# A third open unit of VectorE's exponentials, the table of softmax sums in DRAM, and four weight loads set three tiles apart

## The chip, the cores and the metric

The kernel runs on one core of a Trainium2 chip. The metric is the device time of one execution in microseconds. The engines are TensorE (PE in the profile, with its weight loads as PEld), VectorE (DVE), ScalarE (ACT), GpSimd (POOL) and SyncE (SP), which issues all of the kernel's DMAs from one queue, in program order.

## The reference

One transformer block without biases, in bf16, with 2048 rows of 640 columns, 32 heads of 20 columns and a gated linear part of 1728 columns:

```python
def _A_ref(x, wqkv, wo):
    qkv = (x @ wqkv).reshape(B, S, 3, H, Dh).transpose(2, 0, 3, 1, 4)
    q, k, v = qkv[0], qkv[1], qkv[2]
    scores = jnp.einsum("bhqd,bhkd->bhqk", q, k) * (Dh ** -0.5)
    p = _softmax(scores, axis=-1)
    o = jnp.einsum("bhqk,bhkd->bhqd", p, v)
    return o.transpose(0, 2, 1, 3).reshape(B, S, D) @ wo
def _B_ref(x, w_gate, w_up, w_down):
    h = jnp.einsum("bsd,df->bsf", x, w_gate) * jnp.einsum("bsd,df->bsf", x, w_up)
    return jnp.einsum("bsf,fd->bsd", h, w_down)
x = A_x
h = x + _A_ref(_layernorm(x), A_wqkv, A_wo)
h2 = h + _B_ref(_layernorm(h), B_w_gate, B_w_up, B_w_down)
```

The largest single piece is the exponential of the scores: 32 heads times 2048 times 2048 elements.

## The kernel before, in words

**A written order.** The instruction order on every engine is made at build time. A planner in the kernel keeps modelled times of PE, ACT and DVE (`at["pe"]`, `at["exp"]`, `at["dve"]`) and emits instructions by them. The chip then executes each engine's list in order, with semaphores between the engines.

**Score tiles.** The attention is cut into 683 tiles of up to 1536 score columns (three PSUM banks of 512; two tiles of this kind, `sc`, are in flight). `emit_S` (L577) lets PE make the scores (L591), and ACT takes the exponential of the tile into `E` or `El` (L607). `emit_AV` (L794) multiplies the exponentials with the values, two tiles or more behind (L828), and collects them in one accumulator `acc`. A "segment" is what one accumulator collects: four heads for a block of 512 or 256 query rows. When it is complete, VectorE copies it to an `asb` buffer (L840, three buffers) or adds it to a part (L845).

**Units.** `x_takes` (L627) decides, tile by tile, whether VectorE computes the last bank of the tile in place of ACT; ACT then has 1024 columns instead of 1536. Such a unit is four VectorE instructions on 128x512 elements: `xv<-sc` (L644), which reads the scores, then two polynomial steps `xt` (L654, L655) and `xe` (L649), which gives the exponentials to the AV products. `emit_x` (L636) emits the first at once and puts the other three into `x_open`; `spare` and `step_x` emit these later, between VectorE's other work, as its modelled time allows. With several units open `x_next` alternates between the first two in the list. A unit is taken only if fewer than two units are open, fewer than five are unconsumed (`X_OUT`), VectorE's modelled time is not far behind PE's, and the tile isn't among the last of its segment.

**Work between the tiles.** Projections, the output product, the gated part (`job_glu`) and the down product (`job_y`) are generators that PE runs in the gaps between the tiles; each ends with a VectorE instruction that empties the one PSUM bank `mi`. Where PE has no such work the planner emits matmuls whose result isn't used (`keep_warm`, L509). Layernorm pieces for VectorE wait in the queues `aux` and `hot`. The attention covers the query blocks in turn, and the gated part of each block runs during the attention of the next. The last 256 rows are done after the attention, in `last_tail`.

**Softmax sums.** The sums are rows of the `asb` buffer. `norm` (L693) writes them to DRAM (L700), reads them back spread over 128 partitions into a slice of the SBUF table `sums_all` (L701, 128x512 f32), takes reciprocals (L711), writes these to DRAM (L713) and reads them back broadcast into `bc` (L716); later VectorE multiplies (L719). For eight segments `job_norm` and `last_tail` make the reciprocals by way of PE (`sums_to_rows`, L737) and copy the sums into the table (L745). At the end `flag_ok` (L1468) reduces the whole table (L1471, L1472), to see that all sums were in range.

**The last weights.** When the gated part of the last block's first half has been emitted, `load_last` (L1389) loads the rows of the last 256 positions (`xr`, L1072, 2 x 160 KB) and the first two pairs of weight tiles (`wu`, `wg`, L1202, 4 x 320 KB), one after the other on SP's queue. They are used in `last_tail`.

Of the kernel before, what the change touches and what calls it, by code (L numbers as in the profile page):

```python
# [66 lines left out]
TURN_NS, TURN_FROM = 4200, 2  # L67
HOLD_AT, HOLD_NS = 5300, 450
AV_ROUNDS, AV_LATE, X_LATE = 2, 3, 0
GAP_NS, FILL_LEAST = 250, 300  # L70
FULL_IN, FULL_NS, ALL_NS = 2083, 300, 760
X_LEAST, X_OUT, X_SOON = 2, 5, 4
X_CHUNK = 3
PE_NS = {"out": 6000, "glu": 23000, "y": 7000}
NF_NS = 1800
ALONE_NS = {"out": 4350, "glu": 15260, "y": 5710}
# [16 lines left out]
def kernel(  # L93
# [43 lines left out]
    half = const.tile([P, TPB], F32, name="half")  # L137
    wo = [const.tile([P, D], BF16, name=f"wo{g}") for g in range(NG)]
    N_SUMS = 16 * (NB * NG)
    sums_all = const.tile([P, N_SUMS], F32, name="sums_all")  # L140

    qa = [qkp.tile([P, QA], BF16, name=f"qa{g}", tag=f"qa{g}") for g in range(NG)]
    qb = [qkp.tile([P, QB], BF16, name=f"qb{g}") for g in range(NG)]
# [218 lines left out]
    x_open = deque()  # L362
    x_last = [None]
    holds = deque()
    x_left = {}
    x_put = []
    x_live = deque()
# [30 lines left out]
    def later(n, fn):  # L398
        events.append((now["i"] + n, fn))
# [73 lines left out]
    def spare(until):  # L473
        while True:
            soon = x_open and last_tile[x_open[0][0]] - now["i"] <= X_SOON
            if at["dve"] + (x_next()[0] if soon or x_open and not aux else 600) > until + TOL:
                break
            if step_aux(hot):
                continue
            if soon:  # L480
                step_x()
            elif not step_aux() and not step_x():
                break
# [143 lines left out]
    def x_takes(i):  # L627
        us, n = tiles[i]
        s = us[-1][0]
        whole = segs[s][4] == "only"  # L630
        if not whole and (aux or last_tile[s] - i < X_CHUNK):
            return False
        return (n == EW and (PASS[segs[s][0]][0] < LAST_B or room()) and last_tile[s] - i >= X_LEAST and len({u[0] for u in us if not whole and u[3] >= n - BANK or whole}) == 1
                and len(x_open) < 2 and at["dve"] < at["pe"] + PE_DVE + TOL and len(x_live) < X_OUT)

    def emit_x(ps, us):  # L636
        s = us[0][0]
        w = PASS[segs[s][0]][2]
        v = xp.tile([P, BANK], F32, name="xv", bufs=2)
        u = v[:].bitcast(U16).rearrange("p (n h) -> p n h", h=2)[:, :, 0]  # L640
        t = xp.tile([P, BANK], F32, name="xt", bufs=2)
        e = xp.tile([P, BANK], I16, name="xe", bufs=X_OUT)
        dve(608, 0)
        took = nc.vector.tensor_scalar(v[:], ps, X_SCALE, X_BASE, ALU.mult, ALU.max)  # L644
        x_live.append((s, us[-1][1], us[-1][2]))
        x_left[s] = x_left.get(s, 0) + 1

        def last():
            nc.vector.scalar_tensor_tensor(e[:], t[:], X_R, v[:], ALU.mult, ALU.add)  # L649
# [3 lines left out]
        x_open.append((s, deque([  # L653
            lambda: nc.vector.scalar_tensor_tensor(t[:], u, X_P, u, ALU.add, ALU.mult),  # L654
            lambda: nc.vector.scalar_tensor_tensor(t[:], t[:], X_Q, u, ALU.add, ALU.mult),  # L655
            last])))
        x_last[0] = x_open[-1]
        return took
# [31 lines left out]
    def read_out(b):  # L690
        return all(("om", b, t) in done for t in TAILS[b])

    def norm(s, asb):  # L693
        p, g = segs[s][0:2]
        b, c0, w = PASS[p]
        n = w // 32
        r16 = sums_all[:, col["n"]:col["n"] + n]
        col["n"] += n
        sums = dram.tile([HPG, w], F32, name="sums", tag=f"sums{w}")
        nc.sync.dma_start(sums[:], asb[DH:P:SLOT, 0:w])  # L700
        nc.sync.dma_start(r16, sums[:].rearrange("j (c f) -> (j c) f", f=n))  # L701

        due = at["dve"] + SUMS_NS

        def back():
            if at["pe"] < due and now["i"] < n_tiles:
                later(1, back)
                return
            ri = nrm.tile([P, n], F32, name="ri", tag=f"ri{n}")
            dve(130)  # L710
            nc.vector.reciprocal(ri[:], r16)  # L711
# [6 lines left out]
            def times(asb, bc, p, g, c0, w):  # L718
                nc.vector.tensor_tensor(On[g][:, c0:c0 + w], asb[:, 0:w], bc[:, 0:w], ALU.mult)  # L719
# [14 lines left out]
            nc.tensor.matmul(ps[:, HPG * t:HPG * (t + 1)], lhsT=asb[:, t * P:(t + 1) * P], rhs=identf[:, DH:P:SLOT], start=True, stop=True)  # L734
        return ps

    def sums_to_rows(ps, w):  # L737
        n = w // SLOT
        r16 = sums_all[:, col["n"]:col["n"] + n]
        col["n"] += n  # L740
# [4 lines left out]
        nc.vector.tensor_copy(r16, ps[:, 0:n])  # L745
        return bc

    def rows_to_cols(bc, w, ps):
# [4 lines left out]
    def job_norm(s, asb):  # L753
        p, g = segs[s][0:2]
        b, c0, w = PASS[p]
        ps = sums_on_pe(asb, w)
        yield 780 * w // QB
        dve(700, 0)
        bc = sums_to_rows(ps, w)
# [5 lines left out]
        nc.vector.tensor_tensor(On[g][:, c0:c0 + w], asb[:, 0:w], ps[:, 0:w], ALU.mult)  # L765
        done.add(("n", p, g))
        yield NEXT

# [25 lines left out]
    def emit_AV(upto):  # L794
# [41 lines left out]
        if acc["left"] == 0:  # L836
            dve(605 if w == QB else 342, 0)
            if kind in ("copy", "only"):
                asb = parts[g] if kind == "copy" else nrm.tile([P, QB], F32, name="asb", bufs=3)
                nc.vector.tensor_copy(asb[:, 0:w], acc["t"][:, 0:w])  # L840
                if kind == "copy":
                    part[g] = asb
            else:
                asb = part[g]
                nc.vector.tensor_tensor(asb[:, 0:w], acc["t"][:, 0:w], asb[:, 0:w], ALU.add)  # L845
            acc["seg"], acc["from"], at["acc"] = None, now["i"] + 2, at["dend"] + DVE_PE
            if s == FINAL:
                final["asb"] = asb
            elif (p, g) in FAST:
                opens["nf", p, g] = at["dend"] + DVE_PE  # L850
                urgent.append((("nf", p, g), job_norm(s, asb)))
            elif kind in ("only", "last"):
                norm(s, asb)
# [535 lines left out]
    def load_last():  # L1389
        st = tail_st[LAST_B]  # L1390
        load_tail(st, LAST_T)
        load_w(0, st)
        load_w(1, st)

    def run(gen):
        for _ in gen:
# [2 lines left out]
    def last_tail():  # L1399
# [16 lines left out]
                                 rhs=wo[NG - 1][:, hf * HALF:(hf + 1) * HALF], start=False, stop=True)  # L1416
        ta, tb = LAST_T
        out_most(ta, 0)
        bc = sums_to_rows(sums_on_pe(asb, HW), HW)
        out_most(ta, 1)  # L1420
        ps = rows_to_cols(bc, HW, accp.tile([P, QB], F32, name="acc"))
        for k in range(2):
# [41 lines left out]
    def fill():  # L1464
        while step() is not None:
            pass

    def flag_ok():  # L1468
        n = col["n"]
        bits = sums_all[:, 0:n].bitcast(I32)  # L1470
        nc.vector.tensor_reduce(ext[:, 0:1], bits, axis=AX.X, op=ALU.min)  # L1471
# [165 lines left out]
```

## Time and profile before

| | |
|---|---|
| median of 3 runs | 899.88 us (899.21 to 900.29) |
| the profiled execution | 895.79 us |
| its span from first to last instruction | 893.9 us |
| mean granted TensorE clock | 0.997 |
| busy in the span | PE 836.4 us, DVE 778.4, ACT 851.4, POOL 31.5 |
| tiles' exponentials on ACT (L607) | 683 instructions, 482 with 1536 columns or less than a full tile, 201 with 1024 |
| units on VectorE (L644) | 201 |

Durations are those of the profiled execution, whose time is 4.09 us below the median of the runs. In groups of instructions a line gives the engine, the operation, output and input by the program's names, shapes and the count, then busy time in us and the mean in ns, then the engine's idle time just before these instructions with what ended most of it. A timeline row gives start and duration in us, with the idle time before it in brackets; a row with a count stands for several neighbouring instructions, shown with the shape of the first. PEclk is the granted TensorE clock as a share of full speed.

### The profile page before, as it was taken

Reading aid. Unit: us, or ns where it says so; the run is one execution under the profiler, and the core shown is the slowest. Engines: PE = TensorE matmul, PEld = TensorE weight load, DVE = VectorE, ACT = ScalarE, POOL = GpSimd, SP = SyncE. Lnnn points to the kernel's source line nnn. Section 1 sums busy time; section 2 is a strip of 40 time slices with the busy share of each in tenths; the row PEclk is TensorE's granted clock in tenths of the full one; section 3 lists DMA queues with packets and bytes.
Section 4 is the critical chain, followed back from the end, with each engine's and each line's share of the span. In section 5 each row is a group of like instructions: output and inputs, shape, how many; then the busy total and the mean of one; then the engine's idle time right before and its main releaser. Section 6 shows DMA issues by size and latency. Waiting matters only on the chain.

```text
span 893.9 us, 22151 instructions
## 1 busy us (share of the span) xinstructions
PE 836.4 (94%) x9006; PEld 377.0 (42%) x9006; DVE 778.4 (87%) x1458; ACT 851.4 (95%) x719; POOL 31.5 (4%) x122
## 2 busy tenths in 40 slices
PE   8999999999998999999999999988999999899897
PEld 5333232222233445444444554333544554455365
DVE  7779988999999998998998899999889998988752
ACT  6999999999999999999999999999999999999851
POOL 4100000000002000001000000000001000000000
PEclk9999999999999999999999999999999999999999
DMA  6130011010133465431315252001563121010310
GB/s 199 30 44 17 2 29 25 18 47 14 33 109 102 121 194 157 132 93 27 98 45 124 74 134 65 8 23 31 133 162 79 52 66 30 2 43 15 90 37 19
DMA packets 112244, 60.83 MB, mean 68 GB/s; under 512 B 38948, under 2 KB 109132, under 8 KB 112136
## 3 DMA queue, kind: packets, MB, share of 16 engines
q1 hardware_dynamic: 112136, 59.36, 25.5%
q8 instruction: 72, 1.18, 0.5%
q14 instruction: 36, 0.29, 0.1%
HBM read 48.78 MB, written 7.27 MB: 63 GB/s over the span
## 4 chain that ended last, share of the span: by engine, by line
ACT 58%; PE 20%; issue 13%; DVE 6%; DMA 2%; SPq 0%; ACTq 0%; DVEq 0%
ACT E L607 48%; ACT El L607 10%; PE sc L591 4%; PE mi L1254 3%; PE acc L828 3%; PE f L1236 2%; PE mi L1303 2%; PE mi L509 1%; PE f L1303 1%; PE mi L307 1%; DMA sums<-asb 1%; PE mi L1085 1%; PE mi L322 1%; DVE xv L644 1%; DMA wg<-in_B_w_gate_dram 1%
## 5 line engine op out<-in xcount | busy, mean ns | idle before, releaser
L607 ACT ACTIVATE E<-sc 128x1536 bf16<-128x1536 f32 (+1 forms) x559 | 693.9, 1394 | 4.4 <-PE sc L591 3.9
L591 PE MATMUL sc<-qa,kT 32*128 32x256 bf16 (+1 forms) x2176 | 202.9, 318 | 16.5 <-ACT E L607 9.8
L591 PEld LDWEIGHTS <-kT 32*128 32x128 bf16 x3136 | 85.0, 91 | 223.1 <-issue 191.1
L828 PE MATMUL acc<-E,vx 128*32 128x256 bf16 (+1 forms) x2243 | 174.8, 316 | 1.0 <-ACT E L607 0.7
L644 DVE TENSOR_SCALAR xv<-sc 128x512 f32<-128x512 f32 x201 | 138.4, 689 | 40.9 <-PE sc L591 37.0
L607 ACT ACTIVATE El<-sc 128x1536 bf16<-128x1536 f32 (+1 forms) x124 | 159.8, 1367 | 0.5 <-PE sc L591 0.4
L649 DVE SCALAR_TENSOR_TENSOR xe<-xt,xv 128x512 int16<-128x512 f32 x201 | 135.6, 680 | 0.7
L655 DVE SCALAR_TENSOR_TENSOR xt<-xt,xv 128x512 f32<-128x512 f32 x201 | 135.3, 681 | 0.5
L654 DVE SCALAR_TENSOR_TENSOR xt<-xv 128x512 f32<-128x512 uint16 x201 | 134.8, 682 | 0.3
L828 PEld LDWEIGHTS <-vx 128*32 128x32 bf16 x3136 | 62.3, 95 | 83.6 <-issue 77.9
L307 PE MATMUL mi<-lnT,wp 128*128 128x512 bf16 x305 | 84.8, 381 | 4.3 <-DVE qa L314 1.8
L591 PE MATMUL sc<-qb,kT 32*128 32x256 bf16 (+1 forms) x960 | 68.8, 281 | 5.1 <-ACT E L607 2.9
L1303 PE MATMUL mi<-wd,hh 128*128 128x320 bf16 x378 | 65.1, 301 | 0.0
L828 PE MATMUL acc<-El,vx 128*32 128x256 bf16 (+1 forms) x576 | 64.3, 295 | 0.0
L1254 PE MATMUL mi<-ln2T,wg 128*128 128x256 bf16 x410 | 59.3, 274 | 3.9 <-DVE u L1259 2.3
L509 PE MATMUL mi<-kT,ident 128*128 128x512 bf16 x192 | 58.5, 387 | 3.4 <-DVE xr L1307 2.2
L1254 PE MATMUL mi<-ln2T,wu 128*128 128x256 bf16 x410 | 57.8, 274 | 2.6 <-DVE hh L1262 1.6
L828 PE MATMUL acc<-xe,vx 128*32 128x256 bf16 (+1 forms) x317 | 59.0, 305 | 0.0
L1303 PEld LDWEIGHTS <-hh 128*128 128x128 bf16 x448 | 37.8, 98 | 28.2 <-issue 16.8
L1254 PEld LDWEIGHTS <-wg 128*128 128x128 bf16 x410 | 35.5, 97 | 24.9 <-issue 19.5
L1254 PEld LDWEIGHTS <-wu 128*128 128x128 bf16 x410 | 35.7, 97 | 21.9 <-issue 17.9
L307 PEld LDWEIGHTS <-wp 128*128 128x128 bf16 x310 | 24.5, 97 | 43.8 <-issue 30.7
(152 smaller groups left out, 619.9 us busy)
## 6 DMA issues: line engine op xcount, KB each, us to landing
wu<-in_B_w_up_dram SPq DMA_DIRECT2D x38, 320.0 KB
wg<-in_B_w_gate_dram SPq DMA_DIRECT2D x38, 320.0 KB
bc<-scr SPq DMA_DIRECT2D x60, 64.0 KB
bc<-scr SPq DMA_DIRECT2D x104, 32.0 KB
qsp<-qa SPq DMA_DIRECT2D x8, 384.0 KB
xr<-in_A_x_dram SPq DMA_DIRECT2D x16, 160.0 KB
out_dram<-xr SPq DMA_DIRECT2D x14, 160.0 KB
wd<-in_B_w_down_dram SPq DMA_DIRECT2D x13, 160.0 KB
```

Source lines behind the costliest of these rows:

```text
L307: nc.tensor.matmul(ps[:], lhsT=wslice(m, g, c), rhs=lnT[:, c, ch * QB:(ch + 1) * QB], start=(c == 0), stop=(c == KT - 1))
L509: nc.tensor.matmul(ps[:], lhsT=ident[:], rhs=kT[0][:, 0:BANK], start=True, stop=True)
L591: nc.tensor.matmul(sc[:, o:o + w], lhsT=kT[g][SLOT * j:SLOT * (j + 1), kt * P:(kt + 1) * P], rhs=q_of(g, b, c0, w)[SLOT * j:SLOT * (j + 1) ...
L607: exps = nc.scalar.activation(e[:, 0:n_act], sc[:, 0:n_act], ACT.Exp, bias=EXP_BIAS, scale=SM_SCALE)
L644: took = nc.vector.tensor_scalar(v[:], ps, X_SCALE, X_BASE, ALU.mult, ALU.max)
L649: nc.vector.scalar_tensor_tensor(e[:], t[:], X_R, v[:], ALU.mult, ALU.add)
L654: lambda: nc.vector.scalar_tensor_tensor(t[:], u, X_P, u, ALU.add, ALU.mult),
L655: lambda: nc.vector.scalar_tensor_tensor(t[:], t[:], X_Q, u, ALU.add, ALU.mult),
L828: nc.tensor.matmul(acc["t"][SLOT * j:SLOT * (j + 1), 0:w], lhsT=vx[kt][:, VS * h:VS * h + SLOT], rhs=e, start=(acc["n"][j] == 0), stop=(ac ...
L1236: nc.tensor.matmul(ps[:, 0:n], lhsT=st["w", fp][k][:, c, f_cols(fp, f2)], rhs=st["ln2T"][:, c, c0:c0 + n], start=(c == 0), stop=(c == KT - 1))
L1254: nc.tensor.matmul(ps[:, f2 * n:(f2 + 1) * n], lhsT=st["w", fp][k][:, c, f_cols(fp, f2)], rhs=st["ln2T"][:, c, c0:c0 + n], start=(c == 0), ...
L1303: nc.tensor.matmul(ps[:, 0:HALF], lhsT=st["hh"][f // 2][:, f % 2, t * P % HW:t * P % HW + P], rhs=late["Wd"][f][:, cs], start=(f == 0), st ...
```

## The change

Three things are changed. (1) Up to three units may be open (`X_OPEN`) where both `aux` and `hot` are empty; where something waits there the limit stays two. `xv` gets a third buffer; `xt` keeps two, and a unit's `xt` is allocated at its second step. (2) The table of sums moves from SBUF to DRAM. `keep_sums` writes each segment's sums into it, `norm` reads its part back into a small tile `r16`, the eight segments that went by way of PE write theirs by a DMA instead of a VectorE copy, and `read_sums` fetches the whole table (256 KB) into a `bc` buffer in `last_tail`. With it comes a count of `asb` buffers not yet multiplied (`unmade`): before a fourth copy is emitted, waiting `aux` and `hot` pieces are emitted, and while three are unmade units near the end of their segment lose their precedence over those pieces. (3) The four weight tiles of `load_last` are issued 0, 3, 6 and 9 tiles later.

```diff
-GAP_NS, FILL_LEAST = 250, 300
+GAP_NS, FILL_LEAST, LAST_STEPS = 250, 300, 3
+X_OPEN, ASB = 3, 3
...
-    sums_all = const.tile([P, N_SUMS], F32, name="sums_all")
+    sums_all = dram.tile([P * N_SUMS], F32, name="sums", bufs=1)
...
-            if soon:
+            if soon and len(unmade) < ASB:
                 step_x()
...
-                and len(x_open) < 2 and at["dve"] < at["pe"] + PE_DVE + TOL and len(x_live) < X_OUT)
+                and len(x_open) < (2 if aux or hot else X_OPEN) and at["dve"] < at["pe"] + PE_DVE + TOL and len(x_live) < X_OUT)
...
-        v = xp.tile([P, BANK], F32, name="xv", bufs=2)
+        v = xp.tile([P, BANK], F32, name="xv", bufs=X_OPEN)
...
+    def keep_sums(asb, w):
+        n = w // SLOT
+        sums = sums_all[P * col["n"]:P * (col["n"] + n)]
+        col["n"] += n
+        nc.sync.dma_start(sums.rearrange("(j q) -> j q", j=HPG), asb[DH:P:SLOT, 0:w])
+        return sums
     def norm(s, asb):
...
-        r16 = sums_all[:, col["n"]:col["n"] + n]
-        col["n"] += n
-        sums = dram.tile([HPG, w], F32, name="sums", tag=f"sums{w}")
-        nc.sync.dma_start(sums[:], asb[DH:P:SLOT, 0:w])
-        nc.sync.dma_start(r16, sums[:].rearrange("j (c f) -> (j c) f", f=n))
+        sums = keep_sums(asb, w)
+        r16 = nrm.tile([P, n], F32, name="r16", tag=f"r{n}")
+        nc.sync.dma_start(r16[:], sums.rearrange("(q f) -> q f", f=n))
...
-    def sums_to_rows(ps, w):
+    def sums_to_rows(ps, w, asb):
...
+        keep_sums(asb, w)
...
-        nc.vector.tensor_copy(r16, ps[:, 0:n])
...
+                if kind == "only":
+                    while len(unmade) >= ASB and (step_aux(hot) or step_aux()):
+                        pass
+                    unmade.add((p, g))
...
     def load_last():
         st = tail_st[LAST_B]
         load_tail(st, LAST_T)
-        load_w(0, st)
-        load_w(1, st)
+        for fp in range(2):
+            two = st["w", fp] = []
+            for m, src in enumerate((B_w_up, B_w_gate)):
+                later(LAST_STEPS * (2 * fp + m), lambda fp=fp, src=src, nm=("wu", "wg")[m], two=two: two.append(
+                    w_tile(src, fp, late["w"].tile([P, KT * FPW], BF16, name=nm))))
...
-        bc = sums_to_rows(sums_on_pe(asb, HW), HW)
+        bc = sums_to_rows(sums_on_pe(asb, HW), HW, asb)
+        read_sums()
...
+    def read_sums():
+        final["sums"] = nrm.tile([P, N_SUMS], F32, name="bc")
+        nc.sync.dma_start(final["sums"][:], sums_all[:].rearrange("(q f) -> q f", f=N_SUMS))
     def flag_ok():
-        bits = sums_all[:, 0:n].bitcast(I32)
+        bits = final["sums"][:].bitcast(I32)
```

More of the change, by code (lines that the diff above doesn't have):

```diff
@@ L364 @@
     holds = deque()
+    unmade = set()
     x_left = {}
@@ L638, in emit_x, with second @@
         w = PASS[segs[s][0]][2]
-        v = xp.tile([P, BANK], F32, name="xv", bufs=2)
+        v = xp.tile([P, BANK], F32, name="xv", bufs=X_OPEN)
         u = v[:].bitcast(U16).rearrange("p (n h) -> p n h", h=2)[:, :, 0]
-        t = xp.tile([P, BANK], F32, name="xt", bufs=2)
+        t = []
+        def second():
+            t.append(xp.tile([P, BANK], F32, name="xt", bufs=2))
+            nc.vector.scalar_tensor_tensor(t[0][:], u, X_P, u, ALU.add, ALU.mult)
         e = xp.tile([P, BANK], I16, name="xe", bufs=X_OUT)
@@ L648, in last @@
         def last():
-            nc.vector.scalar_tensor_tensor(e[:], t[:], X_R, v[:], ALU.mult, ALU.add)
+            nc.vector.scalar_tensor_tensor(e[:], t[0][:], X_R, v[:], ALU.mult, ALU.add)
             x_left[s] -= 1
@@ L653, in emit_x @@
         x_open.append((s, deque([
-            lambda: nc.vector.scalar_tensor_tensor(t[:], u, X_P, u, ALU.add, ALU.mult),
-            lambda: nc.vector.scalar_tensor_tensor(t[:], t[:], X_Q, u, ALU.add, ALU.mult),
+            second,
+            lambda: nc.vector.scalar_tensor_tensor(t[0][:], t[0][:], X_Q, u, ALU.add, ALU.mult),
             last])))
@@ L710, in back @@
             dve(130)
-            nc.vector.reciprocal(ri[:], r16)
+            nc.vector.reciprocal(ri[:], r16[:])
             scr = dram.tile([HPG, w], F32, name="scr", tag=f"scr{w}")
@@ L718, in times @@
             def times(asb, bc, p, g, c0, w):
+                unmade.discard((p, g))
                 nc.vector.tensor_tensor(On[g][:, c0:c0 + w], asb[:, 0:w], bc[:, 0:w], ALU.mult)
@@ L735, in sums_on_pe @@
         return ps
-    def sums_to_rows(ps, w):
+    def sums_to_rows(ps, w, asb):
         n = w // SLOT
-        r16 = sums_all[:, col["n"]:col["n"] + n]
-        col["n"] += n
+        keep_sums(asb, w)
         ri = nrm.tile([P, n], F32, name="ri", tag=f"ri{n}")
@@ L758, in job_norm @@
         dve(700, 0)
-        bc = sums_to_rows(ps, w)
+        bc = sums_to_rows(ps, w, asb)
         yield NEXT
@@ L765, in job_norm @@
         nc.vector.tensor_tensor(On[g][:, c0:c0 + w], asb[:, 0:w], ps[:, 0:w], ALU.mult)
+        unmade.discard((p, g))
         done.add(("n", p, g))
@@ L838, in emit_AV @@
             if kind in ("copy", "only"):
-                asb = parts[g] if kind == "copy" else nrm.tile([P, QB], F32, name="asb", bufs=3)
+                if kind == "only":
+                    while len(unmade) >= ASB and (step_aux(hot) or step_aux()):
+                        pass
+                    unmade.add((p, g))
+                asb = parts[g] if kind == "copy" else nrm.tile([P, QB], F32, name="asb", bufs=ASB)
                 nc.vector.tensor_copy(asb[:, 0:w], acc["t"][:, 0:w])
@@ L1466, in fill @@
             pass
+    def read_sums():
+        assert col["n"] == N_SUMS
+        final["sums"] = nrm.tile([P, N_SUMS], F32, name="bc")
+        nc.sync.dma_start(final["sums"][:], sums_all[:].rearrange("(q f) -> q f", f=N_SUMS))
     def flag_ok():
[L1469 to L1470 removed]
+        bits = final["sums"][:].bitcast(I32)
         nc.vector.tensor_reduce(ext[:, 0:1], bits, axis=AX.X, op=ALU.min)
```

## The prediction

> **What bounds the kernel now.** I read the page first, then ACT's groups by shape, then VectorE's groups and waits, and at last the timeline of the one place where ACT stands still.
>
> ```profile
> span 893.9 us, 22151 instructions
> PE 836.4 (94%) x9006; PEld 377.0 (42%) x9006; DVE 778.4 (87%) x1458; ACT 851.4 (95%) x719; POOL 31.5 (4%) x122
> ACT  6999999999999999999999999999999999999851
> ...
> L607 ACT ACTIVATE E<-sc 128x1536 bf16<-128x1536 f32 x398 | 562.0, 1518 | 2.4 <-PE sc L591 2.0
> L607 ACT ACTIVATE E<-sc 128x1024 bf16<-128x1024 f32 x161 | 171.3, 1089 | 2.0 <-PE sc L591 1.9
> L607 ACT ACTIVATE El<-sc 128x1536 bf16<-128x1536 f32 x83 | 121.2, 1505 | 0.0
> L607 ACT ACTIVATE El<-sc 128x1024 bf16<-128x1024 f32 x41 | 43.8, 1088 | 0.5 <-PE sc L591 0.4
> ```
>
> Between the opening and the last exponential at about 854 us every slice of ACT reads 9, and over 683 exponentials ACT waited 4.9 us in all. So the attention lasts as long as ACT's list. It gets shorter in two ways only: fewer columns on ACT, or fewer of those 4.9 us. A unit taken over by VectorE turns 1518 into 1089 ns, which is 0.43 us per unit.
>
> PE is no second bound of the same rank: part of its 836.4 us is filler that the planner emits where it has nothing else.
>
> ```profile
> L509 PE MATMUL mi<-kT,ident 128*128 128x512 bf16 x192 | 58.5, 387 | 3.4 <-DVE xr L1307 2.2 <-DVE qb L314 0.6
> ```
>
> **The weights set apart.** Nearly all of ACT's waiting lies in one place. The rows are SP's, VectorE's, PE's and ACT's timelines and the windows around it:
>
> ```profile
> 826.20 0.90 SPq L1072 DMA_DIRECT2D xr<-in_A_x_dram  x2
> 827.20 0.38 SPq L1202 DMA_DIRECT2D wu<-in_B_w_up_dram  x1
> 827.62 0.52 SPq L1202 DMA_DIRECT2D wg<-in_B_w_gate_dram  x1
> 828.24 0.47 SPq L1202 DMA_DIRECT2D wu<-in_B_w_up_dram  x1
> 828.81 0.82 SPq L1202 DMA_DIRECT2D wg<-in_B_w_gate_dram  x1
> 829.73 0.78 SPq L700 DMA_DIRECT2D sums<-asb  x1
> 834.30 0.34 SPq L701 DMA_DIRECT2D sums_all<-sums  x1
> ...
> 827.16 0.42 DVE L840 COPY asb<-acc 128x256 f32<-128x256 f32 x1 [0.15 <-PE acc L828]
> 833.03 0.69 DVE L644 TENSOR_SCALAR xv<-sc 128x512 f32<-128x512 f32 x1
> 836.43 0.20 DVE L711 RECIPROCAL ri<-sums_all 128x8 f32<-128x8 f32 x1 [2.72 <-DMA sums_all<-sums]
> ...
> 837.65 0.59 PE L509 MATMUL mi<-kT,ident 128*128 128x512 bf16 x2 [2.23 <-DVE xr L1307]
> ...
> 838.85 1.02 ACT L607 ACTIVATE E<-sc 128x1024 bf16<-128x1024 f32 x1 [1.90 <-PE sc L591]
> 840.93 3.96 ACT L607 ACTIVATE E<-sc 128x1536 bf16<-128x1536 f32 x3 [1.05 <-PE sc L591]
> ...
> 829.73 4.56 DMA sums<-asb
> 834.30 2.11 DMA sums_all<-sums
> ...
> 830.00:835.00 5.00, 5.00 (x76) 2.31 (x80) 3.58 (x6) 4.85 (x5) 0.00 (x0) 1.00 0.81 205
> 838.00:842.00 4.00, 4.00 (x34) 0.80 (x32) 3.88 (x7) 2.10 (x2) 0.00 (x0) 0.57 0.14 33
> ```
>
> The accumulator copy ends at 827.58 us. Its sums leave only at 829.73, behind the last weight load in SP's queue, and take 4.56 us to land, because four weight tiles and two row tiles (1.6 MB) fill the DMA engines (share 0.81). The reciprocal that needs them stands next in VectorE's list from 833.72; VectorE waits 2.72 us there, behind it a bank of PE isn't emptied, PE stands still for 2.23 us, and ACT loses 1.90 and then 1.05 us, together 2.95. The second of these is PE at a granted clock of 0.57 after the gap.
>
> With the change one weight tile goes out at about 827.2, the others 3, 6 and 9 tiles later, some 4 us apart. The sums can leave at 827.6, 2.1 us earlier. Were both sums' transfers as slow as now (4.56 and 2.11 us), they would be there at 834.3 and 0.6 of the 2.72 us would stay. The longest of SP's waits for such a transfer is this one, the mean a third of it:
>
> ```profile
> SPq L701 <- DMA sums<-asb: 49.1, 37, 4.3
> ```
>
> With 1.3 us in place of 4.3 the wait goes altogether. A later weight tile can still meet the second transfer: 320 KB at the 205 GB/s of the window are 1.6 us (an estimate), within the time won. So of 2.95 us I put down 2.7, with 2.1 to 2.95 as its bounds where the mechanism holds. The late loads cost nothing: the last goes out about 12 us after the first, near 839, and its tile is first read in the final gated part, which begins on the resident `qa` weights:
>
> ```profile
> 864.99 11.08 PE f L1236 x100
> ```
>
> [...]
>
> **The third open unit.** The rows are VectorE's groups and waits in the attention, and two short stretches of its timeline.
>
> ```profile
> L644 DVE TENSOR_SCALAR xv<-sc 128x512 f32<-128x512 f32 x201 | 138.4, 689 | 40.9 <-PE sc L591 37.0
> DVE xv L644 <- PE sc L591: 37.0, 90, 1.8
> ...
> 301.31 0.68 DVE L655 SCALAR_TENSOR_TENSOR xt<-xt,xv 128x512 f32<-128x512 f32 x1
> 301.91 0.68 DVE L654 SCALAR_TENSOR_TENSOR xt<-xv 128x512 f32<-128x512 uint16 x1
> 302.51 0.69 DVE L649 SCALAR_TENSOR_TENSOR xe<-xt,xv 128x512 int16<-128x512 f32 x1
> ...
> 823.13 0.69 DVE L655 SCALAR_TENSOR_TENSOR xt<-xt,xv 128x512 f32<-128x512 f32 x1
> 823.86 0.69 DVE L649 SCALAR_TENSOR_TENSOR xe<-xt,xv 128x512 int16<-128x512 f32 x1
> ```
>
> Steps of two units in turn start 0.60 us apart, those of a lone unit 0.73. A unit therefore costs VectorE about 2.4 us, and VectorE's waits for scores, 37.0 us, would hold at most 15 units, which is 6.6 us of ACT. That is the upper bound. I then counted, along all 201 rows of L644, how many units had begun L644 and not ended L649 at each idle moment over 30 ns before an `xv`: with one open 97 moments with 22.5 us (0.23 each), with none 32 moments with 18.3 us (0.57 each). The first kind is the planner's modelled time running a little ahead of PE and stays with any limit. The second is VectorE out of work, and a third unit is what it lacked. If all 32 become like the others, 32 x 0.34 = 11 us are won, or 4.5 units. I take 4 units, 1.7 us. The limit does bind: of the 442 full tiles after 68 us, 357 had two units open just before their exponential. Where layernorm pieces wait the limit stays, so I round down. The lower bound lies below nothing; it is the first rival.
>
> **The table in memory.** Each `norm` keeps its five kinds of DMA. For eight segments a VectorE copy goes and a DMA comes:
>
> ```profile
> L745 DVE COPY sums_all<-mi 128x8 f32<-128x8 f32 x7 | 1.1, 159 | 0.0
> ...
> 869.96 0.68 DVE L1471 TENSOR_REDUCE ext<-sums_all 128x1 f32<-128x512 int32 x1
> ```
>
> Eight times 0.16 us of VectorE is 1.3 us, half a unit at best; I count nothing. The new DMAs wait on SP for a copy of `asb` that PE's own part of the norm has already waited for. `read_sums` waits in the queue for the last sums to land: issued near 856, it holds back what follows on SP, which in the trace is nothing before 864 (a store and two weight tiles used at the very end). Two transfers at the old bad price of 4.56 end near 866, ahead of the reduction at 869.96; without that cover they would delay VectorE, not PE. The guard on `unmade` adds no instruction. With three `asb` buffers, a fourth copy ahead of its buffer's multiplication in the same engine's list could not have run, so today there are never more than three, and the loop is idle unless the new order brings it on. Behind it would wait the copy, and behind that PE's next accumulator.
>
> **The sum.** 2.7 + 1.7 = 4.4 us off the profiled 895.79 is 891.4; off the median, 4.09 higher, it is 895.5 us.
>
> **Rivals.**
>
> *The third unit comes too late for its segment (slower).* A segment's accumulator can't be copied before its last `xe`. There are 45 such copies into `asb`, all after units begin; one close and one easy end of them follow:
>
> ```profile
> L840 DVE COPY asb<-acc 128x256 f32<-128x256 f32 (+1 forms) x45 | 21.7, 483 | 5.9 <-PE acc L828 5.3
> ...
> 776.96 0.68 DVE L649 SCALAR_TENSOR_TENSOR xe<-xt,xv 128x512 int16<-128x512 f32 x1
> 777.70 0.39 PE L828 MATMUL acc<-xe,vx 128*32 128x256 bf16 x2
> ...
> 826.83 0.27 PE L828 MATMUL acc<-xe,vx 128*32 128x256 bf16 x1
> ```
>
> The slack was 0.1 us in the first and 2.3 us in the second (its `xe` is the row of 823.86). A third open unit puts up to three more steps, 1.8 us, ahead of that. It decides from the point where the slack is under 1.8 us. If half of the 45 ends are, by 0.9 us on average, and the second score tile hides 0.6 of it (an estimate: 40% of the 1518 ns of one exponential), ACT loses 22 x 0.3 = 7 us; against 4.4 won the time is 902.5. For it: ACT has no reserve at all, and the planner's times are models. Against it: before, no `acc<-xe` product waited at all, units near the end go first, and `emit_AV` may hold the last products back for several tiles.
>
> *Units give nothing.* VectorE takes them earlier, but not more of them: 899.88 - 2.7 = 897.2.
>
> *The stall stays or turns up elsewhere.* All orders shift, and another short chain (sums, reciprocals, `bc`) may meet another load; one such meeting costs 2.95 us here, and with 1.7 of units won and a little lost the time is about 899.5.
>
> **Chances.** The forecast 0.44, units nothing 0.18, stall elsewhere 0.12, slower 0.26. A measurement of this kernel can tell about 0.2%, 1.8 us, from no change; forecast and second rival lie beyond it on the fast side. Faster 0.62, same 0.12, slower 0.26. The range goes from 892.0 (2.95 us and about 11 units) to 903.0, a little past the slower rival's value; the forecast alone would be 892.0 to 897.0.
>
> **What would show it.** `ri` near 836 us without a wait, no TensorE clock under 1 there, `xv` about 205 times with idle below 30 us before it, ACT's 1024-column count up by as much, and the last exponential near 849. It would be wrong if ACT's waits for `sc` add up to more than 5 us, if PE waits ahead of `acc<-xe`, or if `xv` counts 201 or fewer.

## The result, and the profile after

| | before | after |
|---|---|---|
| median of the runs compared | 900.09 us (898.59 to 900.95) | 909.33 us (907.55 to 912.33) |
| ratio, 95% interval | 1 | 1.0107 [1.0087, 1.0127] |
| the profiled execution | 895.79 us | 910.62 us |
| units on VectorE | 201 | 210 |
| last exponential of the attention ends | 853.8 us | 868.6 us |
| from there to the end of the span | 40.1 us | 40.2 us |

The kernel became slower by 1.07%. 895.5 us had been forecast, in a range of 892.0 to 903.0; the sign was wrong, and the time lies above the range. The whole loss lies in the attention: the tail behind the last exponential is as long as before.

The page after: span, busy times, ACT's and PE's clock's slices, the chain that ended last, and two groups.

```profile
span 908.8 us, 22034 instructions
...
PE 835.4 (92%) x8961; PEld 376.1 (41%) x8961; DVE 797.5 (88%) x1486; ACT 850.3 (94%) x719; POOL 32.6 (4%) x122
...
ACT  6999999899999999999999999998999999999941
...
PEclk9999999899999999999989999999999999999999
...
ACT 42%; PE 30%; DVE 15%; issue 10%; DMA 3%; SPq 0%; DVEq 0%; ACTq 0%
...
L650 DVE TENSOR_SCALAR xv<-sc 128x512 f32<-128x512 f32 x210 | 144.7, 689 | 35.3 <-PE sc L593 32.2
```

VectorE did take more units, 210 for 201, and idles less ahead of them (35.3 us for 40.9). ACT is nevertheless no longer the unbroken chain: it holds 42% of it, PE and VectorE have 45% together, and between the opening and the end two of ACT's slices and two of the clock's read 8, the first of each where the time reaches 159 us. ACT's groups by shape and ACT's and PE's waits after the change (us in total, times, longest):

```profile
L609 ACT ACTIVATE E<-sc 128x1536 bf16<-128x1536 f32 x392 | 553.5, 1506 | 15.4 <-PE sc L593 8.4 <-PE acc L839 6.5
L609 ACT ACTIVATE E<-sc 128x1024 bf16<-128x1024 f32 x169 | 178.8, 1081 | 3.0 <-PE acc L839 1.8 <-PE sc L593 1.0
...
ACT E L609 <- PE sc L593: 9.4, 13, 2.5
ACT E L609 <- PE acc L839: 8.2, 6, 3.0
...
PEld L1269 <- DMA wg<-in_B_w_gate_dram: 3.7, 3, 1.7
PE mi L1269 <- DMA ln2T<-ln: 2.4, 2, 1.3
PEld L1269 <- DMA ln2T<-ln: 1.4, 1, 1.4
```

The idle time before `E` was 2.4 and 2.0 us before the change. Now it is 15.4 and 3.0, and one kind of wait is new: `E` waiting for `acc`, 8.2 us, where before there was none. An exponential writes into one of a few `E` buffers (six early, eight later); a buffer is free again when the AV product has read it. ACT waits for `acc` when all are full because PE hasn't multiplied them.

The working against time is the following. One full tile back to back takes ACT 1.33 us, one of 1024 columns 0.913. Measured against such an unbroken list, ACT was 13.9 us behind at its last exponential before, and 32.1 after: 18.2 us more. The nine further units save 9 x 0.417 = 3.75 us. The difference, 14.5 us, is nearly the 14.8 us by which the last exponential ends later.

### The profile page after: what moved, and what is told of

Same layout as the page of the kernel before. It is cut to its first block, busy times and chain, and to the rows that moved or that the text cites. A ratio compares the mean times of both kernels' runs of the same rounds, so it can differ in the third digit from the quotient of the medians.

```text
span 908.8 us, 22034 instructions
## 1 busy us (share of the span) xinstructions
PE 835.4 (92%) x8961; PEld 376.1 (41%) x8961; DVE 797.5 (88%) x1486; ACT 850.3 (94%) x719; POOL 32.6 (4%) x122
## 3 DMA queue, kind: packets, MB, share of 16 engines
q8 instruction: 72, 1.18, 0.6%
## 4 chain that ended last, share of the span: by engine, by line
ACT 42%; PE 30%; DVE 15%; issue 10%; DMA 3%; SPq 0%; DVEq 0%; ACTq 0%
ACT E L609 33%; ACT El L609 9%; PE sc L593 7%; PE mi L1269 5%; PE acc L839 5%; PE mi L308 4%; PE mi L1318 2%; DVE xv L650 2%; DVE xt L647 2%; DVE xt L661 2%; PE f L1251 2%; DVE xe L655 2%; DVE kT L315 1%; PE mi L323 1%; DVE qa L315 1%
## 5 line engine op out<-in xcount | busy, mean ns | idle before, releaser
L650 DVE TENSOR_SCALAR xv<-sc 128x512 f32<-128x512 f32 x210 | 144.7, 689 | 35.3 <-PE sc L593 32.2
L609 ACT ACTIVATE El<-sc 128x1536 bf16<-128x1536 f32 (+1 forms) x122 | 156.2, 1356 | 2.0 <-PE sc L593 1.8
L655 DVE SCALAR_TENSOR_TENSOR xe<-xt,xv 128x512 int16<-128x512 f32 x210 | 141.5, 680 | 0.6
L661 DVE SCALAR_TENSOR_TENSOR xt<-xt,xv 128x512 f32<-128x512 f32 x210 | 140.5, 681 | 0.2
L647 DVE SCALAR_TENSOR_TENSOR xt<-xv 128x512 f32<-128x512 uint16 x210 | 140.0, 682 | 0.1
L839 PEld LDWEIGHTS <-vx 128*32 128x32 bf16 x3136 | 66.0, 95 | 86.3 <-issue 81.4
L308 PE MATMUL mi<-lnT,wp 128*128 128x512 bf16 x305 | 87.5, 385 | 5.4 <-DVE qa L315 2.9
L839 PE MATMUL acc<-xe,vx 128*32 128x256 bf16 (+1 forms) x330 | 62.6, 307 | 0.0
L839 PE MATMUL acc<-El,vx 128*32 128x256 bf16 (+1 forms) x562 | 59.1, 295 | 0.0
L511 PE MATMUL mi<-kT,ident 128*128 128x512 bf16 x142 | 43.2, 386 | 2.5 <-DVE qa L315 0.9
```

Source lines behind the costliest of these rows:

```text
L308: nc.tensor.matmul(ps[:], lhsT=wslice(m, g, c), rhs=lnT[:, c, ch * QB:(ch + 1) * QB], start=(c == 0), stop=(c == KT - 1))
L511: nc.tensor.matmul(ps[:], lhsT=ident[:], rhs=kT[0][:, 0:BANK], start=True, stop=True)
L609: exps = nc.scalar.activation(e[:, 0:n_act], sc[:, 0:n_act], ACT.Exp, bias=EXP_BIAS, scale=SM_SCALE)
L647: nc.vector.scalar_tensor_tensor(t[0][:], u, X_P, u, ALU.add, ALU.mult)
L655: nc.vector.scalar_tensor_tensor(e[:], t[0][:], X_R, v[:], ALU.mult, ALU.add)
L661: lambda: nc.vector.scalar_tensor_tensor(t[0][:], t[0][:], X_Q, u, ALU.add, ALU.mult),
```

## The experiments

In all of them the rest is the change as it stands, unless the diff says otherwise. Each ratio is to runs of the kernel before that were taken beside it, with its 95% interval.

**Two open units at most, and the spacing alone.** Two theories stood: the third unit delays the ends of segments, or the shifted order alone (table, spacing) makes new meetings on SP's queue.

```diff
 # e1_two_open
-                and len(x_open) < (2 if aux or hot else X_OPEN) and ...
+                and len(x_open) < 2 and ...
 # e2_spaced_only: the kernel before, with the later(3 * (2 * fp + m), ...) loop in load_last
 # e3_unspaced
-GAP_NS, FILL_LEAST, LAST_STEPS = 250, 300, 3
+GAP_NS, FILL_LEAST, LAST_STEPS = 250, 300, 0
```

> Everything of the change but the third unit: the limit is two open units always; table in DRAM, guard and spaced weights stay. It takes 201 units, as before. If the third unit is what costs (theory 1), the time is at or below before: 897 to 900 us, and ACT's waits for sc and acc in the attention come to under 3 us. If the table in DRAM and its extra DMAs on SP's queue cost (theory 2), it stays at 905 to 910 us with weights and transposes landing late.

> The kernel before with only the four weight loads set 3 tiles apart. By the prediction the 2.72 us wait of VectorE near 836 us and the slow clock after it go: 897.2 us, 0.3% faster (ratio 0.9965 to 0.998). If the stall only moves, the ratio is 1.000 with a wait of over 2 us elsewhere after 826 us. If the spacing is what costs in the change (theory 3), it is slower than before, 903 us or more.

> The whole change but with the four weight loads issued at once again. Theory 1 and theory 2: as slow as the change or up to 3 us slower, 908 to 913 us. Theory 3 (spacing costs): 900 us.

Measured: e1_two_open 0.9945 [0.9925, 0.9966] (893.14 us), e2_spaced_only 0.9956 [0.9939, 0.9972] (895.05 us), e3_unspaced 1.0141 [1.0097, 1.0185]. e1 is faster than either theory expected. The change without its third unit has the lowest ratio of all versions, and beats both kernels. The spacing alone gives nearly all of that; between e1 and e2, which differ in the table, the intervals overlap, so no cost of the table in memory shows. The instruction lists settle the rest of the second theory: in the traces VectorE's and ACT's instructions come in the same sequence in the kernel before, in e1 and in e2, except for the eight table copies that e1 lacks and its last reduction, which reads `bc`. The table, its guard and the spacing therefore move no order on these two engines; whatever order the change shifts there, it shifts through the third unit. Without the spacing the change is no better (the interval of e3 takes in most of the change's own). The place of the old stall, in SP's, VectorE's and ACT's timelines of e2_spaced_only and its windows (span; busy and count of PE, PEld, DVE, ACT, POOL; clock, DMA share, GB/s):

```profile
831.54 0.38 SPq L1202 DMA_DIRECT2D wu<-in_B_w_up_dram  x1
831.97 0.51 SPq L700 DMA_DIRECT2D sums<-asb  x1
835.41 0.33 SPq L701 DMA_DIRECT2D sums_all<-sums  x1
...
382.69 0.20 DVE L711 RECIPROCAL ri<-sums_all 128x8 f32<-128x8 f32 x1 [1.74 <-DMA sums_all<-sums]
...
837.95 0.19 DVE L711 RECIPROCAL ri<-sums_all 128x8 f32<-128x8 f32 x1
...
848.66 1.45 ACT L607 ACTIVATE E<-sc 128x1536 bf16<-128x1536 f32 x1 [0.62 <-PE sc L591]
...
835.00:840.00 5.00, 5.00 (x71) 2.19 (x64) 4.89 (x10) 4.85 (x6) 0.00 (x0) 1.00 0.62 168
840.00:845.00 5.00, 4.43 (x52) 1.45 (x54) 4.37 (x8) 5.00 (x5) 0.00 (x0) 1.00 0.29 75
```

The sums leave right behind one weight tile instead of four. The reciprocal at 837.95 has no wait in brackets any more, ACT is busy for 9.85 of 10 us, and the clock is 1.00 there. The old stall is gone. A small one follows it: from 847.17 us (842.24 in e1) the clock is at half for 3.41 us, and ACT waits 0.62 and 0.25 us for scores, where it had waited 2.95. The row at 382.69 is a wait of the old kind that the trace of the kernel before doesn't have, though VectorE's and ACT's sequences are the same: single waits come and go between executions, and this profiled one, at 898.09 us, was the longest of e2's seven.

**Where the third unit hurts.** What did the third unit do in the first part, where `E` has six buffers? ACT's and VectorE's timelines and PE's AV products about the first copy into `asb`, after:

```profile
148.98 9.25 ACT L609 ACTIVATE E<-sc 128x1536 bf16<-128x1536 f32 x7
161.19 1.45 ACT L609 ACTIVATE E<-sc 128x1536 bf16<-128x1536 f32 x1 [2.95 <-PE acc L839]
...
156.87 0.68 DVE L655 SCALAR_TENSOR_TENSOR xe<-xt,xv 128x512 int16<-128x512 f32 x1
157.51 0.75 DVE L315 TENSOR_SCALAR qa<-mi,shift_row 128x512 bf16<-128x512 f32 x1
158.18 0.68 DVE L731 TENSOR_TENSOR on<-qa,bc 128x512 bf16<-128x512 f32 x1
158.78 0.69 DVE L661 SCALAR_TENSOR_TENSOR xt<-xt,xv 128x512 f32<-128x512 f32 x1
159.38 0.68 DVE L650 TENSOR_SCALAR xv<-sc 128x512 f32<-128x512 f32 x1
159.98 0.68 DVE L855 COPY asb<-acc 128x512 f32<-128x512 f32 x1
...
159.48 0.39 PE L839 MATMUL acc<-xe,vx 128*32 128x512 bf16 x1
160.71 0.62 PE L839 MATMUL acc<-E,vx 128*32 128x512 bf16 x8 [0.84 <-DVE asb L855]
...
158.00:162.00 4.00, 2.18 (x15) 0.59 (x15) 3.86 (x7) 1.05 (x2) 0.00 (x0) 1.00 0.02 6
```

and the same segment's copy in e1_two_open:

```profile
153.83 10.06 ACT L609 ACTIVATE E<-sc 128x1536 bf16<-128x1536 f32 x8
...
154.29 0.69 DVE L855 COPY asb<-acc 128x512 f32<-128x512 f32 x1
```

Read from below: ACT waits at 161.19 for AV products that begin at 160.71; these wait 0.84 us for the copy of `acc`; the copy stands at 159.98, behind the last `xe` of the segment, with two steps of other units and two other jobs between them, and the product of that `xe` comes only at 159.48, 1.9 us after it. With two units the copy came at 154.29 and ACT ran on without a gap. PE doesn't stand in front of `acc<-xe` with a wait. Instead the product is put behind other work in its list, and what fills up meanwhile are the `E` buffers. Over the whole kernel the time from the start of a unit's `xv` to the end of its `xe` grew from 6.15 to 7.67 us in the median and from 8.25 to 10.39 in the 90th per cent (201 and 210 pairs).

Experiments on this: the third unit only far from a segment's end, only in the first 150 tiles, only after them, and a seventh `E` buffer in the first 160 tiles in the same order.

```diff
-                and len(x_open) < (2 if aux or hot else X_OPEN) and ...
+  # e4_third_far:   (2 if aux or hot or last_tile[s] - i < 6 else X_OPEN)
+  # e6_third_early: (2 if aux or hot or i >= 150 else X_OPEN)
+  # e7_third_late:  (2 if aux or hot or i < 150 else X_OPEN)
...
     # e5_seventh_e; e9_early_seventh_e is this and e6 (identf moves to make the room)
+    re = tc.alloc_tile_pool(name="re", bufs=1, side="right")
...
+        e7["n"] += 1
+        if e7["n"] % 7 == 0 and now["i"] < 160:
+            return re.tile([P, EW], BF16, name="Er")
...
     # e10_soon_8: units within 8 tiles of their segment's end go first
-X_LEAST, X_OUT, X_SOON = 2, 5, 4
+X_LEAST, X_OUT, X_SOON = 2, 5, 8
```

> The whole change, but the third unit only where the segment has at least 6 tiles to go; it takes 201 units in all, as before. If the loss comes from units that end too late for their segment's accumulator (theory 1, in the form of the first rival), ACT's waits for E buffers (releaser PE acc, 8.2 us in the changed kernel) fall below 1 us and the time is 899 to 903 us. If any third unit costs, because all of VectorE's other work comes later, it is 905 to 909 us. If theory 2 holds, 908 us.

> The whole change in its own order of instructions, with a seventh E buffer for the first 160 tiles (and the f32 identity made later, to have room). Theory 1a (a late unit holds the one accumulator, the next segment's products wait, the six E buffers fill, ACT stops): ACT's waits for PE acc before 200 us, 4.45 us in the changed kernel, go, and the slow clock at 164 to 171 us with them, about 6 us in all: 902 to 904 us. If ACT then only waits for the next thing (theory 1b, PE and VectorE are too slow there in any case), 907 us or more.

> The whole change, but a third unit only in the first 150 of 683 tiles; 201 units in all. Theory 1: against the kernel with two units (893.1) it has the early stalls for E buffers and no more units: 898 to 901 us. If the third unit harms only where the gated part and its loads run beside (after 250 us), 893 to 895 us.

> The whole change, but a third unit only from tile 150 on; 205 units. Theory 1: two of the five longer waits for E buffers and the late weights and transposes, less 4 units (1.7 us): 898 to 903 us. If the harm is all in the early part: 891 to 893 us.

> The third unit in the first 150 tiles only (as in the run before last, 904.6 us, 1.0067 of before), with a seventh E buffer for the first 160 tiles; the order of instructions is otherwise that of that run. Theory 1a: its early waits for PE acc (4.45 us) shrink to under 2 us and the time falls by 2.5 to 5 us, to 900 to 902 us (ratio 1.001 to 1.004). Theory 1b (PE and VectorE are what is short there): the ratio stays at 1.006 or more.

> The whole change, but a unit is put ahead of the layernorm and norm pieces from 8 tiles before the end of its segment, not from 4; 198 units. Theory 1a: units end earlier, ACT's waits for PE acc fall from 8.2 us to under 3 us, and in spite of 12 units fewer (5 us of ACT) the time is 903 us or less. If lateness of units isn't the cause: 911 us or more, for the lost units.

Measured: e4 1.0046 [1.0023, 1.0068] (201 units), e5 1.0107 [1.0081, 1.0133] (210), e6 1.0067 [1.0045, 1.0089] (201), e7 0.9990 [0.9970, 1.0010] (205), e9 1.0054 [1.0027, 1.0081] (201), e10 1.0069 [1.0043, 1.0095] (198). ACT's waits for `acc` after the change between 100 and 200 us, and the same for e5_seventh_e:

```profile
ACT E L609 <- PE acc L839: 4.5, 3, 3.0
```

```profile
ACT E L615 <- PE acc L845: 1.6, 1, 1.6
```

So the wait is for `E` buffers: with one more and the same order it falls from 4.5 to 1.6 us in that stretch, and at tile 160 ACT is 5.2 us behind instead of 9.8. In the two profiled executions these 4.6 us are still there at the last exponential (26.9 us behind instead of 32.1). The runs don't confirm it: the ratio stayed at 1.0107 (908.28 us), and e5's profiled execution, at 905.2, was the shortest of its six, the change's, at 910.62, one of its longer ones. Between e6 and e9, which lies between its two expectations, the same buffer brings 0.13%, inside both intervals. So the buffer shortens the wait, and that this saves time is not shown. The third unit late in the attention (e7) measured less than early (e6), although e6 has no unit more than the kernel before; but both ratios lie within what two open units gave in other orders (0.9945 to 1.0068, next part), so a difference between early and late isn't shown either. e6 lies above both of the ranges expected of it. Keeping the third unit from the segments' ends (e4) leaves 0.8 us of waits for `acc`, and the kernel is still slower than before. Putting units first earlier (e10) leaves 3.9 us, where under 3 was expected, at 903.67 us.

**Is it the order by itself?** Every edit to when units are taken also shifts the order of the other work. Controls: two units, and one constant of the planner set a little differently; then the change itself with the same constants.

```diff
-WARM_LATE, NEXT_DVE = 0, 300
+WARM_LATE, NEXT_DVE = 0, 280              # e8_two_other_order: two units
-TOL, LEAST, MARGIN = 200, 216, 20
+TOL, LEAST, MARGIN = 190, 216, 20         # e12_two_other_order_b: two units; f1_three_tol190: three
+TOL, LEAST, MARGIN = 210, 216, 20         # f3_two_tol210: two units; f2_three_tol210: three
-GAP_NS, FILL_LEAST, LAST_STEPS = 250, 300, 3
+GAP_NS, FILL_LEAST, LAST_STEPS = 240, 300, 3   # f6_two_gap240: two units; f5_three_gap240: three
```

> A control: two units, table and spacing as in the changed kernel, but one planner constant moved (NEXT_DVE 280 in place of 300), which shifts the order a little and keeps 201 units. If the order of the kernel before is a lucky one and any shift costs (theory 4), it loses 0.5% or more against the kernel with two units: 898 us or more. If the third unit itself costs, it stays at 892 to 896 us.

> A second control: two units, table and spacing as in the changed kernel, TOL 190 in place of 200, 202 units. Theory 4 (any other order than the one before costs, as the first control's 0.6% against the kernel with two units says): 897 to 901 us. If the first control was unlucky, 892 to 895 us.

> The whole change with TOL 190, the same shift as in the second control; 206 units. If the third unit itself costs (theory 1), it is slower than the same shift with two units (1.0068 of before) by 0.7% or more: 1.014 or over. If what costs is that the order is another one than before, whichever (theory 4), it lies among the other shifted orders, 1.000 to 1.010.

> The whole change with TOL 210; 207 units. Theory 1: slower than the next run by 0.7% or more. Theory 4: within 0.5% of the next run, on either side.

> A third control: two units, table and spacing as in the changed kernel, TOL 210; 200 units. Theory 4: 1.000 to 1.010 of before, as the first two controls (1.0006 and 1.0068). If these two were unlucky: 0.994 to 0.998.

> The whole change with GAP_NS 240 in place of 250; 205 units. The pairs so far, three units against two in the same shift, gave +1.6%, -0.3% and +1.9%. If the third unit costs on average by about 1% (theory 1 weakened), it is slower than the next run by 0.5 to 1.5%. If only luck decides (theory 4): within 0.4% of it or below.

> The fourth control: two units, table and spacing as in the changed kernel, GAP_NS 240; 201 units. Two-unit orders so far: 0.9945, 1.0006, 1.0068, 0.9965 of before. Both theories: 0.994 to 1.007.

| constants | two units | three units | three less two |
|---|---|---|---|
| as they stand | 0.9945 [0.9925, 0.9966] (e1) | 1.0107 [1.0087, 1.0127] | +1.62% |
| `TOL` 190 | 1.0068 [1.0046, 1.0089] (e12) | 1.0037 [1.0018, 1.0056] (f1) | -0.31% |
| `TOL` 210 | 0.9965 [0.9946, 0.9985] (f3) | 1.0158 [1.0131, 1.0186] (f2) | +1.93% |
| `GAP_NS` 240 | 1.0016 [0.9997, 1.0035] (f6) | 1.0047 [1.0027, 1.0068] (f5) | +0.31% |
| mean | 0.9999 | 1.0087 | +0.9% |

e8 (two units, `NEXT_DVE`) measured 1.0006 [0.9989, 1.0023]. Constants alone move the kernel with two units by up to 1.2%; the third unit costs 0.9% in the mean of four pairs, with -0.3 to +1.9% between them. Three of the four pairs point the same way, and their mean is only about 1.7 times its standard error (an estimate from the spread of the four), so four pairs suggest the direction and leave the size open. Of the runs themselves, f2 came out as theory 1 expects, f1 and f5 as theory 4, and e12 lies above both ranges expected of it. The first pair also has the order with the lowest ratio of the five that two units were given, that of the kernel before; the other three pairs alone give 0.6%. The new wait is no peculiarity of three units either: about 784 us it also appears in e8, with two. PE, VectorE and ACT there:

```profile
783.70 0.39 PE L839 MATMUL acc<-xe,vx 128*32 128x256 bf16 x2
784.43 0.41 DVE L855 COPY asb<-acc 128x256 f32<-128x256 f32 x1
784.90 0.40 PE L839 MATMUL acc<-E,vx 128*32 128x256 bf16 x8 [0.80 <-DVE asb L855]
785.37 1.94 ACT L609 ACTIVATE E<-sc 128x1024 bf16<-128x1024 f32 x2 [2.05 <-PE acc L839]
```

In the profiled executions ACT waited for `acc` 8.2, 1.2, 5.9 and 7.3 us with three units (rows of the table in turn, `E` and `El`), and 0.0, 1.1, 0.6 and 3.2 us with two.

**The read of the sums in SP's queue.** A second kind of new wait is that of PE for gated weights and `ln2T` (8.4 us in all after, 2.0 before). SP's queue after, near 541 us, and PE:

```profile
541.11 0.51 SPq L703 DMA_DIRECT2D sums<-asb  x1
543.86 0.34 SPq L712 DMA_DIRECT2D r<-sums  x1
544.26 0.43 SPq L1217 DMA_DIRECT2D wg<-in_B_w_gate_dram  x1
...
547.62 0.22 PEld L1269 LDWEIGHTS <-wg 128*128 128x128 bf16 x3 [1.75 <-DMA wg<-in_B_w_gate_dram]
```

The read at 543.86 waits for the write before it, 2.2 us between them without an issue, and the weight tile stands behind that wait. The experiment issues the read from GpSimd's queue: for the change (e11) and for the two-unit order with `TOL` 190 (f4).

```diff
-        nc.sync.dma_start(r16[:], sums.rearrange("(q f) -> q f", f=n))
+        nc.gpsimd.dma_start(r16[:], sums.rearrange("(q f) -> q f", f=n))
```

> The whole change in its own order, but the read of the sums (r16) is issued from GpSimd's queue, so that weights and transposes on SP's queue aren't held up by the wait for the sums to land. Theory 5 (of the loss after 250 us, the part in which PE waits for weights and ln2T, some 5.5 us in the changed kernel, comes from that wait in SP's queue): 903 to 906 us, ratio 1.003 to 1.007. If the late loads have another reason, 908 to 911 us as the change.

> The second control (two units, TOL 190) with the read of the sums issued from GpSimd's queue. Theory 5 (in a shifted order the loads behind that read on SP's queue come late, with two units as with three): PE's waits for wg and ln2T, 6.5 us in the second control, fall under 2 us and the ratio goes from 1.0068 to 1.000 to 1.004. If the queue isn't the reason there, it stays at 1.005 to 1.009.

Measured: e11 1.0068 [1.0046, 1.0091], f4 1.0070 [1.0046, 1.0094] against 1.0068 without the move. The waits of e11_read_on_pool:

```profile
ACT E L609 <- PE acc L839: 8.1, 5, 3.0
ACT E L609 <- PE sc L593: 6.6, 12, 1.0
DVE ri L722 <- DMA r<-sums: 4.9, 4, 2.0
...
PEld L1269 <- DMA wu<-in_B_w_up_dram: 0.2, 1, 0.2
```

PE's wait for weights is gone (8.4 to 0.2 us), the waits for `acc` stay at 8.1, and 4.9 us of waiting at the reciprocals come instead of 1.3. The ratio is 0.4% lower than the change's, with overlapping edges of the intervals. In the other order the move brings nothing; the waits for `wg` and `ln2T` fell to 3.5 us there, not under 2. So this queue wait is real, and costs the change at most a few tenths of a per cent.

## Why the prediction was wrong, by its steps

**(a) The weights set apart: right.** The stall goes as described. The clock still falls to half once behind that place, at a price of 0.87 us in e2, so the sign "no TensorE clock under 1 there" held only up to 847 us. Two readings were too wide: this place has about two thirds of ACT's 4.9 us of waits, not nearly all, and the weight tiles don't keep 4 us apart (in the changed kernel the second and third leave at 850.13 and 850.61, both behind the read of the sums). e2_spaced_only measured -0.44%, 4.0 us, with 2.5 to 5.5 us in its interval; 2.7 us had been put down. In the changed kernel itself the sums also leave right behind one weight tile (848.09 after 844.75), and the reciprocal at 855.71 has no wait. The 0.57 of the row from 838 to 842 us, in which the prediction places the 1.05 us, is a clock of 0.50 for 3.41 us from 838.27; more on such stretches below.

**(b) The third unit: the gain was right in kind, its price was the failed step.** Idle moments of VectorE with no unit open fell from 18.3 to 7.9 us (19 moments), which is what the step rested on, and nine units came of it, more than twice the four put down: 3.75 us of ACT. The term in the sum held this gain alone, 1.7 us, and nothing for the later ends of the units. In their place the runs showed units that take 7.67 us instead of 6.15 and ACT waiting 8.2 us for `E` buffers; with the limit back at two (e1) both that wait and the 1.62% were gone. Two sentences failed. The first is "before, no `acc<-xe` product waited at all": that was true before and stayed true, and it shows nothing, because the planner moves the product back in PE's list and no wait appears. The second, "`emit_AV` may hold the last products back for several tiles", was used as an argument against the loss; holding them back is the loss, since the products behind them hold the `E` buffers. I had counted as reserve only the second score tile ("0.6 hidden") and not asked how many `E` buffers there are and who releases them.

**(c) The table in memory: right at 0, as far as can be told.** e1 and e2 differ by 0.1%, within the intervals. `read_sums` was issued later than I had said, because all is later, and still lands in time:

```profile
869.95 0.48 SPq L703 DMA_DIRECT2D sums<-asb  x1
871.58 0.34 SPq L1490 DMA_DIRECT2D bc<-sums  x1
...
884.95 0.68 DVE L1494 TENSOR_REDUCE ext<-bc 128x1 f32<-128x512 int32 x1
```

The reduction follows 13 us behind, without a wait. With two units the guard moved nothing, as the unchanged sequences show; whether it ever emitted a piece in the changed kernel was not tested by itself.

**The rivals.** The slower one was the right one by its place (the units' late ends) and by its sign, but with 902.5 us its price was too low and its path was another: not short waits of 0.3 us at 22 ends, but six waits of up to 3.0 us at a few ends where the buffers run full. Of the 18.2 us that ACT fell further behind, these are 8.2 and the longer waits for scores (11.2 us for 4.3, `E` and `El`) 6.9; the other 3.1 I did not resolve. Of the 11.2 us, 5.7 end inside the three stretches at half clock before 860 us (last section). How much of the loss the clock makes by itself, and how much of it would come without the third unit, no run separates. "The stall turns up elsewhere" was priced at one meeting of 2.95 us; the controls show that the order alone moves a kernel with two units by up to 1.2%, some 11 us, from the order that e1 shares with the kernel before. No other price was so far off. The 1.62% between e1 and the change came with the third unit and the order that it made. If the mean of the pairs is taken, about 0.9% of it would come with a third unit in any order and the rest would be the luck of this one; with pairs from -0.3 to +1.9% that split is not shown.

**What would show it.** Of the signs of being wrong the first came: ACT's waits for `sc` above 5 us had been named, and they were 9.4 (with `El` 11.2). The second, a wait ahead of `acc<-xe`, did not appear, though the mechanism did. Of the signs of being right, `xv` came to 210 and not 205, with 35.3 us before it where below 30 was named, and the last exponential ended at 868.6, not near 849.

## What to carry to other kernels

When a side engine may hold more pieces of work open, ask first when each piece ends, not how many it takes: with alternating steps every open piece ends later (7.67 us after its start here, for 6.15), and what is freed by the last of them (here one accumulator, and through it the exponentials' buffers) decides. A wait that the trace doesn't show at the consumer may have been moved into the order by the planner, so look at the next buffer that fills. And where an order comes from a planner, run at least three or four neighbouring orders of both versions before a difference of 1% is put down to the edit.

## What the runs showed of the hardware

PE's half clock was more frequent than I had expected: 17.1 us of it before 860 us in the changed kernel, 3.4 us in the kernel before, and in the changed kernel it also came without a gap as long as the 2.23 us of the prediction's row (the longest in the 3.41 us ahead of its four stretches were 1.36, 0.75, 1.14 and 0.51 us). Windows of after: the 3.41 us ahead of a half-clock stretch, the stretch, and what follows it; then most of another stretch.

```profile
454.69:458.10 3.41, 2.64 (x23) 1.11 (x19) 3.38 (x8) 3.41 (x4) 0.00 (x0) 1.00 0.67 179
458.10:464.93 6.83, 6.83 (x37) 2.63 (x36) 4.37 (x9) 4.81 (x5) 0.00 (x0) 0.50 0.02 7
464.93:468.00 3.07, 3.07 (x28) 1.31 (x24) 2.24 (x5) 2.83 (x3) 0.00 (x0) 0.99 0.00 0
...
164.60:171.40 6.80, 6.26 (x31) 1.20 (x31) 4.73 (x8) 5.56 (x6) 0.00 (x0) 0.50 0.00 0
```

PE was busy 2.64 of the 3.41 us ahead (0.77), its longest gap there 0.75 us. For 6.83 us the clock was 0.50, and ACT was busy for only 4.81 of them. Apart from the last one at the end of each trace, the half-clock stretches in the traces of before and after were 3.41 us long in the kernel before (from 838.27 us), and 6.83, 6.83, 3.41 and 3.41 us in the changed one (from 164.60, 458.15, 625.40 and 860.92). In e2_spaced_only one began with PE busy 2.73 of 3.41 us, so with no gap over 0.68 us:

```profile
570.70:574.11 3.41, 2.73 (x38) 1.64 (x35) 3.25 (x9) 3.41 (x4) 0.00 (x0) 1.00 0.06 19
574.11:577.52 3.41, 3.05 (x31) 0.68 (x26) 2.77 (x6) 2.91 (x3) 0.00 (x0) 0.50 0.00 0
```

What sets the half clock off the runs leave open, and it is not the busy share of the last 3.41 us alone: ahead of the five stretches of before and after, in their order above, PE was busy for 1.18, 2.05, 2.64, 1.70 and 2.75 us of it, yet in the kernel before it was busy for 2.06 us of the 3.41 from 775.00 and the clock stayed at 1.00:

```profile
775.00:778.41 3.41, 2.06 (x27) 0.92 (x23) 3.28 (x10) 3.41 (x4) 0.56 (x1) 1.00 0.00 0
778.41:782.00 3.59, 3.29 (x54) 1.40 (x54) 3.54 (x7) 3.59 (x4) 0.00 (x0) 1.00 0.02 2
```
